# Attention with a token and channel mixer: seven of nine channel-mixing chunks in Strassen's form

## The chip, the cores and the metric

The kernel runs on one NeuronCore of a Trainium2 chip. The metric is the device time of one execution in microseconds (us). The engines are TensorE (PE in the views, with its weight loads as PEld), VectorE (DVE), ScalarE (ACT), GpSimd (POOL) and SyncE (SP), which issues the DMAs.

## The reference

A causal attention with decay feeds a token mixing and a channel mixing, both with a residual. B = 8 batches, H = 8 heads, S = 576 tokens, D = 64; d_model is 512, d_tok 256, d_ch 1536; everything is fp32.

```python
decay = cum[:, :, :, None] - cum[:, :, None, :]          # cum: running sum of log f
scores = np.where(causal, -1000000000.0, scale * q @ k^T + decay)
attn = softmax(scores) @ v
x = np.ascontiguousarray(attn.transpose(0, 2, 1, 3)).reshape(B, S, H * D)
h = np.maximum(x.transpose(0, 2, 1) @ w_tok1, 0.0) @ w_tok2
u = x + h.transpose(0, 2, 1)
h2 = np.maximum(u @ w_ch1, 0.0) @ w_ch2
return u + h2
```

## The kernel before, in words

**Precision.** Each fp32 operand is held as a high part (rounded to the type that PE multiplies fast, by ACT, helper L572) and a low part (the rest, by DVE, L581 and L584, or by POOL, L578). A product of two operands is three matmuls: high weight by high data, low by high, high by low.

**The attention stage**, some 640 us, runs over 64 heads. For each head the scores go into PSUM (L848), DVE takes the row minimum with the mask added (L855), ACT the exponential (L862), POOL normalizes (L890), PE transposes the probabilities (L904) into PSUM, ACT and DVE split them into high and low (L572, L581), and PE multiplies them by v (L974 to L986) into an accumulator that is folded into x (L1024, L1031). Between these steps stands the mixer of the batch before: transposes of x (L1205), the two products of the token mixing (L1238 to L1241 and the lines behind), and two of the twelve tiles of d_ch of the channel mixing (L1307 and its two neighbours for the first product, L1335 to L1337 for the second, whose sum ACT copies out at L1342). The result of these two tiles is kept in DRAM as `part_d`, u as `u_d`.

**The channel-mixing stage** takes the other ten tiles of d_ch in nine chunks of 512 tokens (`begin`, `up`, `down`, L1070 to L1170). Per chunk, `up` is ten groups of 12 matmuls of 128x512 (L1121 to L1123) into one PSUM bank, from which ACT takes relu and the high part and DVE the low part (L584); `down` is ten groups of 12 matmuls (L1142 to L1144) into four accumulators, which DVE adds to the residual at the chunk's end (L1155). That is 240 matmuls a chunk. `third` decodes the weights of this stage while the first chunks run (L682 and others).

**PSUM** has eight banks, b0 to b7. b0 and b1 are one tile of [128, 1024], `pair0`, that holds scores; b2 and b3 are `pair1`, the attention's accumulator. Their halves are the four accumulators of `down`. b4 to b7 are four tiles `bank4` to `bank7` of [128, 512], which everything of the kind "one" takes in turn: transposes, scores, the mixer's products, `up`.

**What sets the order.** `Plan` (L359) gets every operation with an engine, a cost, a priority and the buffers it uses (`Buf` of a kind; `slots_of` says which pieces of memory serve a kind) and lays out one fixed order for each engine, with a slot for each buffer, by walking through its own clock. The engines then run their orders, and an instruction waits on semaphores for instructions of other engines that use the same tile; those waits are put in when the program is built, from the tiles that its operands belong to, and not by the plan.

Of the kernel before, what the change touches and what calls it, by code (L numbers as in the profile page):

```python
# [15 lines left out]
P = 128  # L16
# [323 lines left out]


# [19 lines left out]
class Plan:  # L361
# [9 lines left out]
    FIFO = ("ring", "xt", "part", "pr", "hl", "k1", "k2", "vv", "raw", "vr", "p34", "p2", "p1", "p0", "low", "hid", "d_raw", "d_g", "qf", "f34", "f2", "f1", "f0")  # L371
# [35 lines left out]
    def run(self, slots):  # L407
# [30 lines left out]
        def place_all(o):  # L438
            got, taken, nx = [], set(), {}
            for b in o.bufs:  # L440
                if b.slot is not None:
                    continue
                k = b.kind
# [4 lines left out]
                for s in slots[k]:  # L448
                    if all(free_at(u, o.eng) <= t and u not in taken for u in s):
                        break  # L450
                else:
                    return None
                got.append((b, s))
                taken.update(s)
            return got

        while left:
            moved = False
            for e, lst in ready.items():
# [71 lines left out]
def build(nc, env, dims):  # L531
# [112 lines left out]
    def decode(prio, loads, w, hi, lo, tok, late=None):  # L644
# [35 lines left out]
        def s6():  # L680
# [4 lines left out]
        p.op("DVE", d_dve(w, True), prio, s2, wr=[gb], bufs=[gb], port=True)  # L685
        p.op("DVE", d_dve(w, True), prio, s3, rd=[gb], wr=[(gb, 1)], bufs=[gb], port=True)
        p.op("DVE", d_dve(w), prio, s4, port=True, rd=rd, wr=[(gb, 1)], bufs=[rb, gb])
        p.op("DVE" if late else "POOL", d_dve(w) if late else d_ptt(w), prio, s5, port=True, rd=[(gb, 1)], wr=[gb], bufs=[gb])
        p.op("DVE", d_dve(w), prio, s6, port=True, rd=rd, wr=[gb], bufs=[rb, gb])
# [3 lines left out]
            rd=[gb, (tok, "h")], wr=[(tok, "l")], bufs=[gb], port=True,  # L693
# [7 lines left out]
    def dec_list():  # L701
# [31 lines left out]
        def rest(i, which):  # L733
            def go(prio):
# [3 lines left out]
                else:  # L738
# [4 lines left out]
                    late=f"gate{int(i >= PAIRS0)}",  # L743
# [300 lines left out]
    DB = PRM["DB"] if F1 else 0  # L1044
    whole = [(x * HS, HS, True) for x in range(2 * DB)]
    rest_, n_ch = N - DB * S, -(-(N - DB * S) // 512)
    cuts = [DB * S + x * rest_ // n_ch for x in range(n_ch + 1)]
    part_ = [(x, y - x, False) for x, y in zip(cuts, cuts[1:])]
    chunks = part_ + whole if PRM["DLAST"] else whole + part_
# [20 lines left out]
    def begin(g, ch):  # L1070
# [16 lines left out]
        hl = [(Buf("ring"), Buf("ring")) for c in range(NC)]  # L1087
# [14 lines left out]
    hid = {}  # L1102

    def up(g, ch, i):
# [5 lines left out]
        hid[ch, i] = hb  # L1110

# [15 lines left out]
        p.op("PE", [mm_(w_)] * 12, base + g, mm, rd=[(x, z) for x in ws for z in "hl"] + both, wr=[ps], bufs=[ps, *both, hb])  # L1127
# [3 lines left out]
    def down(g, ch, i):  # L1131
# [4 lines left out]
        for c in range(NC):  # L1136
# [10 lines left out]
            p.op("PE", [mm_(w_)] * 3, base + g + 1.5, mm, rd=[(wk, "h"), (wk, "l"), (hb, 0), (hb, 1)], wr=[acc[c]], bufs=[acc[c], hb])  # L1147
# [15 lines left out]
    steps = [(ch, i) for ch, x in enumerate(chunks) for i in range(0 if x[2] else F1, NF)]  # L1163
    for g, s_ in enumerate(steps):
        if g == 0:
            up(0, *s_)
        if g + 1 < len(steps):
            up(g + 1, *steps[g + 1])
        down(g, *s_)
    return p  # L1170


# [188 lines left out]
def slots_of():  # L1361
# [6 lines left out]
    for kind in ("raw", "vr", "hl", "k1", "k2", "vv", "pr", "p34", "p2", "p1", "p0", "low", "ring", "part", "xt", "d_raw", "d_g"):  # L1368
# [11 lines left out]
def attn_mixer_kernel(  # L1380
# [51 lines left out]
    for _ in range(3):  # L1432
        nc.tensor.matmul(E["one"][("b4",)], ident, mask[:, :512], start=True, stop=True)
# [8 lines left out]
    tiles(mixp, "d_raw", [P, C, 2], U32, n_("d_raw"))  # L1442
    tiles(mixp, "d_g", [P, 2, C], U32, n_("d_g"))
    tiles(mixp, "part", [P, S], F32, n_("part"))
# [29 lines left out]
    def swap(x):  # L1474
# [49 lines left out]
```

## Time and profile before

| | |
|---|---|
| median of 3 runs | 1133.28 us (1130.95 to 1133.99) |
| span of the profiled execution | 1133.7 us |
| mean granted clock of TensorE | 0.986 |
| PE busy | 1088.6 us, 96% |
| DVE, ACT, POOL busy | 620.8, 557.9, 525.3 us |
| L1121 to L1123 and L1142 to L1144, 360 matmuls each | 140.0 or 140.1 us each, 389 ns mean |

The profiled execution has no time of its own beside its span; the three runs lie around it. Busy times are of instructions in work; matmuls are pipelined, so that the 389 ns of one overlap the next, and what a matmul adds to a row of them is the pitch from start to start. A view of windows gives the busy time of each engine in each stretch, with the number of instructions in brackets, then the granted clock, the share of the DMA engines and GB/s; restricted to a tile it counts only instructions that touch it. The tile "bank" is bank4 to bank7 together. In the rows of groups stands: line, engine, operation, output and inputs, count, busy us, mean ns, idle time ahead and what ended it. In a timeline a row begins with the start in us and the duration.

### The profile page before, as it was taken

The page shows a single profiled execution, that of the slowest core. Times are in us where ns is not written, and L with a number is a line of the kernel's source. Part 1 is how long each engine was busy: PE and PEld are TensorE (multiplying, and loading weights), DVE is VectorE, ACT ScalarE, POOL GpSimd, SP SyncE. Part 2 cuts the span into 40 slices and gives each one's busy share as a digit, 9 for nine tenths or more (in the row PEclk, how much of TensorE's full clock was granted, in tenths as well). Part 3 has the DMA queues.
Part 4 walks back from the last instruction along what each step waited for, and adds up shares of the span by engine and source line. Part 5 has one row for each costly group of instructions (what it writes and reads, how often), then busy time and mean ns, then how long its engine had stood idle before and what let it go on. Part 6 is the DMA issues. An engine that isn't in the chain of part 4 may idle for free.

```text
span 1133.7 us, 18919 instructions
## 1 busy us (share of the span) xinstructions
PE 1088.6 (96%) x6542; PEld 947.7 (84%) x6542; DVE 620.8 (55%) x1618; ACT 557.9 (49%) x1441; POOL 525.3 (46%) x613
## 2 busy tenths in 40 slices
PE   8988888999999999999998999999999999999998
PEld 5567777899899999889898888888888888888886
DVE  5677687788787787788779894121212121211111
ACT  4676676868788787778786542121111111111110
POOL 4466786768768687687762304130303031211010
PEclk7998999999999999999999999999999999999999
DMA  7576774878677777767752644130303030302011
GB/s 194 132 164 153 164 212 119 220 212 208 164 188 192 201 182 198 184 191 173 192 151 80 210 134 156 48 88 25 112 1 112 1 112 1 112 1 75 19 56 38
DMA packets 70224, 146.67 MB, mean 129 GB/s; under 512 B 10048, under 2 KB 27456, under 8 KB 69104
## 3 DMA queue, kind: packets, MB, share of 16 engines
q1 hardware_dynamic: 70128, 145.45, 47.0%
q8 instruction: 52, 0.85, 0.3%
q14 instruction: 44, 0.36, 0.1%
HBM read 63.46 MB, written 28.31 MB: 81 GB/s over the span
## 4 chain that ended last, share of the span: by engine, by line
PE 76%; DMA 9%; DVE 5%; SPq 3%; POOL 3%; ACT 3%; issue 2%; DVEq 0%; POOLq 0%; ACTq 0%
DMA k<-hl 7%; PE bank L1121 7%; PE bank L1122 7%; PE bank L1123 7%; PE pair L1142 7%; PE pair L1144 7%; PE pair L1143 7%; PE bank L904 6%; PE bank L848 6%; PE pair L848 3%; PE pair L984 2%; PE pair L986 2%; SPq L821 1%; PE bank L1238 1%; PE pair L974 1%
## 5 line engine op out<-in xcount | busy, mean ns | idle before, releaser
L584 DVE SCALAR_TENSOR_TENSOR hid<-bank,hid 128x512 fp32r<-128x512 f32 x90 | 62.2, 691 | 333.5 <-ACT hid L572 332.9
L578 POOL TENSOR_TENSOR ring<-xt,ring 128x512 fp32r<-128x512 f32 (+1 forms) x68 | 91.7, 1364 | 322.9 <-ACT ring L572 322.3
L572 ACT ACTIVATE hid<-bank 128x512 fp32r<-128x512 f32 x90 | 53.9, 599 | 342.3 <-PE bank L1123 342.1
L890 POOL TENSOR_SCALAR pr<-pr,rec 128x576 f32<-128x576 f32 (+4 forms) x320 | 165.0, 536 | 59.1 <-DVE rec L883 36.2
L572 ACT ACTIVATE p<-bank 128x384 fp32r<-128x384 f32 (+3 forms) x300 | 128.2, 474 | 46.4 <-PE bank L904 43.0
L904 PE MATMUL bank<-ident,pr 128*128 128x128 f32 (+1 forms) x960 | 137.0, 276 | 5.6 <-DVE p L581 2.0
L1122 PE MATMUL bank<-ring,w1r 128*128 128x512 f32 x360 | 140.1, 389 | 0.0
L1121 PE MATMUL bank<-ring,w1r 128*128 128x512 f32 x360 | 140.1, 389 | 0.0
L1143 PE MATMUL pair<-hid,w2r 128*128 128x512 f32 x360 | 140.0, 389 | 0.0
L1144 PE MATMUL pair<-hid,w2r 128*128 128x512 f32 x360 | 140.0, 389 | 0.0
L1142 PE MATMUL pair<-hid,w2r 128*128 128x512 f32 x360 | 140.0, 389 | 0.0
L1123 PE MATMUL bank<-ring,w1r 128*128 128x512 f32 x360 | 140.0, 389 | 0.0
L862 ACT ACTIVATE pr<-bank,nmin 128x448 f32<-128x448 f32 (+3 forms) x256 | 118.1, 467 | 40.5 <-DVE nmin L855 38.6
L581 DVE TENSOR_TENSOR p<-bank,p 128x384 fp32r<-128x384 f32 (+1 forms) x180 | 106.3, 595 | 40.6 <-ACT p L572 38.6
L855 DVE CUSTOM_DVE_ANT_0 bank<-bank,mask 128x448 f32<-128x448 f32 (+3 forms) x256 | 107.1, 432 | 36.3 <-PE bank L848 32.7
L904 PEld LDWEIGHTS bank<-ident,pr 128*128 128x128 f32 (+1 forms) x960 | 108.4, 131 | 18.9 <-DVE low L581 3.2
L848 PE MATMUL bank<-k 128*128 128x320 f32 (+1 forms) x480 | 90.0, 315 | 12.3 <-DMA k<-hl 8.9
L848 PEld LDWEIGHTS bank<-k 128*128 128x128 f32 (+1 forms) x480 | 65.4, 182 | 19.9 <-DMA k<-hl 9.0
L1123 PEld LDWEIGHTS bank<-ring,w1r 128*128 128x128 f32 x360 | 67.6, 188 | 14.1
L1143 PEld LDWEIGHTS pair<-hid,w2r 128*128 128x128 f32 x360 | 67.6, 188 | 14.0
L1144 PEld LDWEIGHTS pair<-hid,w2r 128*128 128x128 f32 x360 | 67.6, 188 | 14.0
L1121 PEld LDWEIGHTS bank<-ring,w1r 128*128 128x128 f32 x360 | 67.7, 188 | 13.9
(125 smaller groups left out, 2454.4 us busy)
## 6 DMA issues: line engine op xcount, KB each, us to landing
k<-hl SPq DMA_DIRECT2D x180, 288.0 KB
raw<-in_qk SPq DMA_DIRECT2D x30, 576.0 KB
vr<-in_v SPq DMA_DIRECT2D x32, 320.0 KB
ud<-xt SPq DMA_DIRECT2D x8, 1152.0 KB
pd<-part SPq DMA_DIRECT2D x32, 288.0 KB
out_t<-part SPq DMA_DIRECT2D x36, 256.0 KB
d_raw<-in_w_ch SPq DMA_DIRECT2D x12, 512.0 KB
d_raw<-in_w_ch SPq DMA_DIRECT2D x40, 128.0 KB
```

The lines of the kernel that those rows point to most:

```text
L572: nc.scalar.activation(out, in_, func, scale=scale)
L848: nc.tensor.matmul(ps[:m, of : of + w], k[:, 0, i0 : i0 + m], k[:, 1, j0 : j0 + w], start=(x == 0), stop=(fq or x == 1))
L855: nc.vector.tensor_tensor_reduce(x, x, E["mask"][:m, a : a + w], -1.0 / D**0.5, 3e38, op0=ALU.add, op1=ALU.min, accum_out=E["nmin"][sm][:m ...
L862: nc.scalar.activation(at(pr)[:m, poff[t] : poff[t] + w], at(buf)[:m, of : of + w], AF.Exp, bias=E["nmin"][sm][:m, t : t + 1], scale=-1.0, ...
L890: nc.gpsimd.tensor_scalar(x, x, r, 0.0, op0=ALU.mult, op1=ALU.add)
L904: nc.tensor.transpose(out, at(pr)[:, poff[i] + start[j] : poff[i] + end[j]], E["ident"])
L1121: nc.tensor.matmul(q, wh[:, c, :], h_, start=(c == 0), stop=False)
L1122: nc.tensor.matmul(q, wl[:, c, :], h_, start=False, stop=False)
L1123: nc.tensor.matmul(q, wh[:, c, :], l_, start=False, stop=(c == NC - 1))
L1142: nc.tensor.matmul(q, wh, h_, start=(i == i0), stop=False)
L1143: nc.tensor.matmul(q, wl, h_, start=False, stop=False)
L1144: nc.tensor.matmul(q, wh, l_, start=False, stop=(i == NF - 1))
```

## The change

Two of the nine chunks stay as they are (`CONV = 2`). Seven are computed by `strassen(s)`: the weight matrix and the data of each product are seen as two by two blocks, and seven products of blocks, with sums of blocks, take the place of eight (the form of Strassen's scheme with seven products in `TERMS`). Both matrix products of the chunk are done so. A block of data is 256 tokens wide, so that matmuls are 128x256 where they were 128x512.

In the first product each of the seven terms is made of five groups of six matmuls, each group into half a bank of PSUM. For the first term ACT copies each group out; for the others DVE adds it to one of the four partial results H11 to H22, for one term to two; ACT takes relu of a partial result when it is complete. In the second product a term is 30 matmuls into a whole pair of banks, and DVE adds the sum to one to four quarters of the buffer R, which holds the residual. POOL makes the sums of data blocks, ACT and DVE split them into high and low parts. `prep` makes the sums of weight blocks S1 to S4 once, during the two chunks that stay, on POOL and DVE, each split by ACT and DVE, and puts them where the attention's weights, the spare part of the ring and the old hidden tiles lay.

To make room, memory is laid out anew: the decode buffers become one tile `dd`, in which H11 to H22 lie later; the part buffers one tile `part`, which R takes whole; the attention stage's mixer weights one tile `held`. The eight banks of PSUM become four tiles `pair0` to `pair3` of [128, 1024]; b4 to b7 are their halves. "any" is any half, "two" any whole pair. From the third pair of weights on the decode may run beside POOL (`port`).

The core of the diff:

```diff
+HW = 256
+CONV = 2
...
-    chunks = part_ + whole if PRM["DLAST"] else whole + part_
+    chunks = [(512 * x, 512, False) for x in range(CONV)]
...
+    def prep(w, pr, eng, kind, prio):
...
+        for x, (o_, y, op) in enumerate((("11", "21", ALU.subtract), ("21", "22", ALU.add), ("22", "11", ALU.subtract), ("12", "22", ALU.subtract))):
+            tail(eng, d(HW), prio, lambda o_=o_, y=y, op=op: tt(view(o_), view(o_), view(y), op), rd=[(g, y)], wr=[(g, o_)], bufs=[g])
...
+    for pr in range(PH):
+        prep(1, pr, "DVE" if pr % 2 else "POOL", GT[pr], late - 60 + 4 * pr)
...
+    TERMS = (("11", "A11"), ("21", "A12"), ("T2", "S2"), ("T3", "S3"), ("T4", "A22"), ("T1", "S1"), ("22", "S4"))
+    L = 3.57
+    LO_POOL = (1, 4, 5, 6)
+
+    def strassen(s):
...
+            for pr in range(PH):
+                ps = Buf("any")
...
+                    for c in (0, 1):
+                        cs = slice(c * P, (c + 1) * P)
+                        h_, l_ = v2(at(th))[:, c, :], v2(at(tl))[:, c, :]
+                        nc.tensor.matmul(q, wh[:, cs], h_, start=c == 0, stop=False)
+                        nc.tensor.matmul(q, wl[:, cs], h_, start=False, stop=False)
+                        nc.tensor.matmul(q, wh[:, cs], l_, start=False, stop=c == 1)
...
+                def add(out, a, ps=ps, Hq=Hq):
+                    nc.vector.tensor_tensor(Hq(out), at(ps)[:, :HW], Hq(a), op=ALU.add)
...
+                if k == 0:
+                    tail("ACT", d_act(HW), pp, lambda ps=ps, Hq=Hq: nc.scalar.activation(Hq("21"), at(ps)[:, :HW], AF.Copy), rd=[ps], wr=[(H["21"], pr)], bufs=[ps, H["21"]])
+                for out, a in ((), (("11", "21"),), (("12", "21"),), (("22", "12"),), (("21", "22"),), (("22", "22"), ("12", "12")), (("12", "12"),))[k]:
...
+        def product(k, src, blk, xs):
+            ps = Buf("two")
...
+            to = (QUADS, ("11",), ("12", "21", "22"), ("21", "22"), ("21",), ("12", "22"), ("12",))[k]
+            for q in to:
+                tail(
+                    "DVE", d_dve(512), t2 + L * (k + 1), lambda q=q: nc.vector.tensor_tensor(Rq(q), v(), Rq(q), op=ALU.add),
+                    rd=[ps], wr=[(R, q)], bufs=[ps, R],
+                )
...
+    for s in range(N // 512 - CONV):
+        strassen(s)
...
+    k["any"] = [(f"b{i}",) for i in (4, 5, 6, 7, 0, 1, 2, 3)]
+    k["two"] = pairs
+    k["R"] = [tuple(("part", i) for i in range(4))]
...
-    pairs = [psum.tile([P, 1024], F32, name=f"pair{i}") for i in range(2)]
-    E["sc"] = {("b0", "b1"): pairs[0]}
-    E["av"] = {("b2", "b3"): pairs[1]}
-    E["acc"] = {(f"b{i}",): pairs[i // 2][:, (i % 2) * 512 : (i % 2) * 512 + 512] for i in range(4)}
-    E["one"] = {(f"b{i}",): psum.tile([P, 512], F32, name=f"bank{i}") for i in range(4, 8)}
+    pairs = [psum.tile([P, 1024], F32, name=f"pair{i}") for i in range(4)]
+    E["two"] = {(f"b{2 * i}", f"b{2 * i + 1}"): x for i, x in enumerate(pairs)}
+    E["sc"] = E["av"] = E["two"]
+    E["any"] = {(f"b{i}",): pairs[i // 2][:, (i % 2) * 512 : (i % 2) * 512 + 512] for i in range(8)}
+    E["acc"] = E["one"] = E["any"]
```

How the orders change. Up to about 615 us of the trace of before the instructions of each engine stand in the same order and on the same banks; what differs is the tile that a bank belongs to. bank4 and bank5 are now the halves of pair2, bank6 and bank7 those of pair3. Lines are 13 later for the attention's (L848 is L861, L904 is L917, L572 is L585, L581 is L594), and L1335 is L1587, L1342 is L1594. The names behind the arrow are the inputs; "waits" are the engines whose semaphores the instruction waits for.

PE in the attention, at 512.6 us of the trace. Before:

```order
L986 MATMUL pair1_64<-p341_172,vv1_167 128x256
L1335 MATMUL bank5_66<-ring8_139,w2h_105 128x288 [waits DVE_49]
L1336 MATMUL bank5_66<-ring8_139,w2l_106 128x288
L1337 MATMUL bank5_66<-ring9_140,w2h_105 128x288
L1335 MATMUL bank5_66<-ring10_141,w2h_105 128x288 [waits Activation_49]
...
L1335 MATMUL bank6_67<-ring8_139,w2h_105 128x288 [waits DVE_49]
...
L848 MATMUL bank4_65<-k10_162 128x320 [waits DMAHW2_49,DMAHW0_49,DVE_49]
```

The same place after:

```order
L999 MATMUL pair1_64<-p341_156,vv1_151 128x256
L1587 MATMUL pair2_65<-ring8_130,held_97 128x288 [waits Activation_49]
L1588 MATMUL pair2_65<-ring8_130,held_97 128x288
L1589 MATMUL pair2_65<-ring9_131,held_97 128x288
L1587 MATMUL pair2_65<-ring10_132,held_97 128x288
...
L1587 MATMUL pair3_66<-ring8_130,held_97 128x288 [waits DVE_49]
...
L861 MATMUL pair2_65<-k10_146 128x320 [waits DMAHW2_49,DMAHW0_49,Activation_49]
```

No row has moved. The first matmul into bank 5 waited for DVE, and now waits for ACT, which reads bank 4; the scores into bank 4 waited for DVE, which read bank 4, and now for ACT, which copies bank 5.

ACT at the same place. Before:

```order
L572 ACTIVATE p340_171<-bank5_66 128x384 [waits PE_49]
L572 ACTIVATE p00_176<-bank6_67 64x512 [waits DVE_49,PE_49]
L572 ACTIVATE p20_173<-bank7_68 128x384 [waits PE_49]
L572 ACTIVATE p00_176<-bank7_68 64x64
L572 ACTIVATE p10_175<-bank4_65 128x512 [waits DVE_49,PE_49]
L767 ACTIVATE vv1_167<-vr0_159 128x10x64 [waits DMAHW2_49,PE_49]
L1342 ACTIVATE part0_148<-bank5_66 128x288 [waits DVE_49,PE_49]
```

After:

```order
L585 ACTIVATE p340_155<-pair2_65 128x384
L585 ACTIVATE p00_160<-pair3_66 64x512 [waits DVE_49,PE_49]
L585 ACTIVATE p20_157<-pair3_66 128x384
L585 ACTIVATE p00_160<-pair3_66 64x64 [waits DVE_49]
L585 ACTIVATE p10_159<-pair2_65 128x512 [waits PE_49]
L780 ACTIVATE vv1_151<-vr0_143 128x10x64 [waits DMAHW2_49,PE_49]
L1594 ACTIVATE part_135<-pair2_65 128x288 [waits DVE_49]
```

The order is the same again. The read of 64x64 has a new wait for DVE, which reads the other half of pair3, and the copy at the end now waits for DVE alone, whose instruction there (L594 into p10) reads the other half of pair2 and itself has a new wait for PE.

The first product of a chunk in Strassen's form, on PE and DVE, which has no counterpart before. PE in a term whose groups DVE adds, the first matmuls of its groups:

```order
L1307 MATMUL pair2_65<-ring4_126,w1r1_6974 128x256 [waits Activation_49]
...
L1307 MATMUL pair3_66<-ring4_126,w1r3_7177 128x256 [waits DVE_49]
...
L1307 MATMUL pair2_65<-ring4_126,w1r5_7181 128x256 [waits DVE_49]
...
L1307 MATMUL pair2_65<-ring4_126,w1r7_7185 128x256
...
L1307 MATMUL pair3_66<-ring4_126,w1r9_7189 128x256 [waits DVE_49]
```

Two groups go into the halves of pair2, then one into pair3, and so on; each first one into a pair waits for DVE, which adds what is there.

ACT's copies of the first term of a chunk:

```order
L1323 ACTIVATE dd_134<-pair3_66 128x256 [waits PE_49]
...
L1323 ACTIVATE dd_134<-pair2_65 128x256 [waits DVE_49,PE_49]
L1323 ACTIVATE dd_134<-pair2_65 128x256 [waits PE_49] x3
```

One group of the term lies in pair3 and four in pair2, and each copy waits for PE.

More of the change, by code (lines that the diff above doesn't have):

```diff
@@ L339, with dd_units @@
 F1 = PRM["F1"]
+QUADS = ("11", "12", "21", "22")
+HW = 256
+CONV = 2
+def dd_units(a, n):
+    return tuple(("dd", i) for i in range(a, a + n))
 def asf(ap):
@@ L637, in build, with decode @@
         fill(i)
-    def decode(prio, loads, w, hi, lo, tok, late=None):
+    def decode(prio, loads, w, hi, lo, tok, late=None, port=True):
         rb, gb = Buf("d_raw"), Buf("d_g")
@@ L1086, in begin @@
             of += w
-        hl = [(Buf("ring"), Buf("ring")) for c in range(NC)]
+        hl = [(Buf("ringx"), Buf("ringx")) for c in range(NC)]
         for c in range(NC):
@@ L1100, in begin @@
         st[ch] = (hl, cp, toks, [Buf("acc") for c in range(NC)])
-    hid = {}
+    hid, hids = {}, []
     def up(g, ch, i):
@@ L1161, in down, with tail @@
                 )
-    steps = [(ch, i) for ch, x in enumerate(chunks) for i in range(0 if x[2] else F1, NF)]
+    def tail(*a, **k):
+        return p.op(*a, port=False, **k)
+    steps = [(ch, i) for ch in range(CONV) for i in range(F1, NF)]
+    at_g = lambda g: g + 150 * (g >= F2)
     for g, s_ in enumerate(steps):
@@ L1167, in build @@
         if g + 1 < len(steps):
-            up(g + 1, *steps[g + 1])
-        down(g, *s_)
+            up(at_g(g + 1), *steps[g + 1])
+        down(at_g(g), *s_)
+    PH = F2 // 2
+    late = base + 400
+    held = [((nm, t), z) for nm, n in (("t1", NS), ("w1", NC), ("w2", F1)) for t in range(n) for z in "hl"]
+    held += [(("t2", k, hf), z) for k in range(NT) for hf in range(2) for z in "hl"]
+    tail("POOL", 1, HB + 3, lambda: None, rd=["gate0", "gate1"], wr=["gatec", *held])
+    tail("POOL", 1, HB + 3, lambda: None, rd=[((f"w{w}r", i), z) for w in (1, 2) for i in range(F2) for z in "hl"], wr=["gated"])
@@ L1367, in slots_of @@
     k["one"] = [(f"b{i}",) for i in (4, 5, 6, 7)]
-    for kind in ("raw", "vr", "hl", "k1", "k2", "vv", "pr", "p34", "p2", "p1", "p0", "low", "ring", "part", "xt", "d_raw", "d_g"):
+    k["any"] = [(f"b{i}",) for i in (4, 5, 6, 7, 0, 1, 2, 3)]
+    k["two"] = pairs
+    k["R"] = [tuple(("part", i) for i in range(4))]
+    k["ringx"] = [(("ring", i),) for i in range(8)]
+    k["tr"] = [(("ring", i),) for i in range(5)]
+    k["d_raw"] = [dd_units(4 * i, 4) for i in range(3)]
+    k["d_g"] = [dd_units(12 + 4 * i, 4) for i in range(2)]
+    for i, q in enumerate(QUADS):
+        k["H" + q], k["gt" + q] = [dd_units(5 * i, 5)], [dd_units(5 * i, 4)]
+    for kind in ("raw", "vr", "hl", "k1", "k2", "vv", "pr", "p34", "p2", "p1", "p0", "low", "ring", "part", "xt"):
         k[kind] = [((kind, i),) for i in range(PRM[f"n_{kind}"])]
@@ L1432, in attn_mixer_kernel @@
     for _ in range(3):
-        nc.tensor.matmul(E["one"][("b4",)], ident, mask[:, :512], start=True, stop=True)
+        nc.tensor.matmul(E["any"][("b4",)], ident, mask[:, :512], start=True, stop=True)
     def tiles(pool, kind, shape, dt, n):
@@ L1481, in swap @@
             tiles(wp, "hid", [P, 2, 512], F32R, PRM["n_hid"])
+            spare = wp.tile([P, 512], F32R, name="spare")
             wp.tile([P, 8], F32, name="even1")
+            early = [held[:, i * 512 : (i + 1) * 512] for i in range(held.shape[1] // 512)]
+            early += [spare[:, :]] + [E["ring"][(("ring", i),)][:, :512] for i in (8, 9, 10, 11)]
+            last = [E["ring"][(("ring", i),)][:, :512] for i in (6, 7)]
+            last += [x[:, j, :] for x in E["hid"].values() for j in (0, 1)]
+            E["piece"] = [("gatec", x) for x in early] + [("gatee", x) for x in last]
     E["swap"] = swap
```

232 lines of the change are left out of this document (203 added, 29 removed).

## The prediction

> **What bounds the kernel now.** I read the page's busy times and the cores first, then the windows of 100 us, then the same windows for the tile bank alone, then single rows.
>
> ```profile
> PE 1088.6 (96%) x6542; PEld 947.7 (84%) x6542; DVE 620.8 (55%) x1618; ACT 557.9 (49%) x1441; POOL 525.3 (46%) x613
> core 0: 1133.7 us, clock 0.986
> ```
>
> Windows, all work (stretch, us, then PE, PEld, DVE, ACT, POOL, clock, DMA share, GB/s):
>
> ```profile
> 300.00:400.00 100.00, 99.10 (x762) 95.03 (x761) 79.56 (x233) 80.66 (x227) 71.20 (x84) 1.00 0.68 182
> 640.00:700.00 60.00, 60.00 (x274) 50.05 (x273) 49.54 (x89) 25.84 (x44) 9.27 (x8) 1.00 0.42 136
> 700.00:760.00 60.00, 60.00 (x267) 49.69 (x266) 11.00 (x17) 9.99 (x18) 16.42 (x14) 1.00 0.30 92
> ```
>
> TensorE (PE) bounds both stages. From about 640 us the nine chunks run with PE full and the others nearly idle. Before, in the attention, PE is busy 99.10 of 100, but VectorE (DVE) and ScalarE (ACT) stand at 80: there the three live by handing PSUM banks around quickly. So I ask two questions: what the chunks save on PE, and whether the banks are still handed around as fast. The profiled execution is the 1133.7 us span; the median of the runs, 1133.28, is 0.4 lower, and I sum against 1133.7 without correcting.
>
> **Seven products for eight.** A chunk has 240 matmuls of 128x512 now and 420 of 128x256 then. The pitch of the first is 60 / 267 = 0.2247 us (700 to 760 above), so 53.9 us a chunk. That of the second is in the attention, where six such matmuls stand in a row:
>
> ```profile
> 320.48 0.28 PE L1238 MATMUL bank<-ring,t1h 128*128 128x256 f32 x1
> ...
> 321.08 0.29 PE L1241 MATMUL bank<-ring,t1h 128*128 128x256 f32 x1
> ```
>
> Five pitches are 0.60, so 0.12 each and 50.4 us a chunk: 3.5 less, times seven **-25 us**. A rounding of 0.0025 in the pitch is 1 us a chunk, so -32 to -18. The Trainium skill (TensorE: Matmul & The Clock Gate, "Wait — 56ns, not 53.3ns?") has a warm matmul at its columns over 2.4 GHz plus 2.5 ns; by that a chunk would go from 51.8 to 45.9 us and the seven would save 41. This trace is slower than that rule by 9 to 11 ns a matmul in both sizes, so the row stands.
>
> The other engines must feed this. The nearest rows:
>
> ```profile
> L581 DVE TENSOR_TENSOR ring<-bank,ring 64x256 fp32r<-64x256 f32 x16 | 6.7, 418 | 1.3 <-ACT ring L572 0.9
> L584 DVE SCALAR_TENSOR_TENSOR hid<-bank,hid 128x512 fp32r<-128x512 f32 x90 | 62.2, 691 | 333.5 <-ACT hid L572 332.9
> L572 ACT ACTIVATE hid<-bank 128x512 fp32r<-128x512 f32 x90 | 53.9, 599 | 342.3 <-PE bank L1123 342.1
> L572 ACT ACTIVATE ring<-bank 64x256 fp32r<-64x256 f32 x16 | 6.0, 376 | 0.1
> L578 POOL TENSOR_TENSOR ring<-xt,ring 128x512 fp32r<-128x512 f32 x36 | 46.0, 1298 | 303.6 <-ACT ring L572 303.4
> L578 POOL TENSOR_TENSOR w1l<-d_g,w1h 128x256 fp32r<-128x256 f32 x4 | 2.9, 735 | 2.0 <-ACT w1h L572 1.9
> ```
>
> DVE per chunk: 35 adds out of PSUM and 35 low parts at 0.418, 3 low parts and 14 adds at 0.691: 41 us. ACT: 60 operations of 256 at 0.376 and 7 of 512 at 0.599: 27. GpSimd (POOL): 20 of 512 at 1.298 and 4 of 256 at 0.735: 29. All fit under 50 us of PE: no bound by load. The residual's buffer R is single, so its load waits for the chunk before to store its last quarter, but is needed only when the first matrix product, 210 matmuls or 25 us, is done: nothing. The weight combinations (ten preparations, about 29 us of DVE and 33 of POOL) fall into the two chunks kept, of some 54 us each, where DVE has 10.5 and then 49 free of 60, POOL 44: hidden, **+2** (0 to 8, if the decode before them is late). At the end one add follows the last matmul in place of four: **-1**.
>
> **The PSUM tiles.** The diff also makes bank4 to bank7 halves of two pair tiles, and that reaches into the attention. What sharing a tile does is visible now, in the last chunk, whose accumulators are halves of pairs:
>
> ```profile
> 1126.69 0.39 PE L1144 MATMUL pair<-hid,w2r 128*128 128x512 f32 x1
> 1127.37 0.39 PE L1144 MATMUL pair<-hid,w2r 128*128 128x512 f32 x1
> 1127.87 2.65 DVE L1155 TENSOR_TENSOR part<-pair,part 128x512 f32<-128x512 f32 x4 [2.83 <-PE pair L1144]
> ```
>
> The first add needs only the half finished by 1127.08 (1126.69 + 0.39), but starts 0.11 after the other half's last matmul ends at 1127.76. Two engines take turns on a pair, whichever halves they touch. In the changed order the attention's instructions stand in the same order as before, but have such waits on pair2 and pair3, as the rows ahead show. One turn, in the trace of before:
>
> ```profile
> 512.17 1.07 ACT L572 ACTIVATE p<-bank 128x384 fp32r<-128x384 f32 x3
> 512.71 0.30 PE L1335 MATMUL bank<-ring,w2h 128*128 128x288 f32 x1
> 513.37 0.30 PE L1337 MATMUL bank<-ring,w2h 128*128 128x288 f32 x1
> 513.57 0.67 DVE L581 TENSOR_TENSOR p<-bank,p 128x512 fp32r<-128x512 f32 x1
> 513.75 0.40 ACT L1342 ACTIVATE part<-bank 128x288 f32<-128x288 f32 x1
> 514.54 0.40 PE L848 MATMUL bank<-k 128*128 128x320 f32 x1
> ```
>
> The third ACT operation reads bank 4 until 513.24; the six matmuls fill bank 5 beside it; DVE reads bank 4, ACT copies bank 5, the scores go into bank 4. As halves of one pair they queue. With 0.05 us for a handoff (a choice; the add above took 0.11), the matmuls start at 513.29 (+0.58), the sixth ends 0.58 later than its 513.67, DVE starts at 514.30 (+0.73), ACT at 515.02 (+1.27), the scores at 515.47 (+0.93). Queued behind that wait on PE is everything, since PE goes in order: transposes, the other heads' products, then ACT and DVE that wait for these.
>
> I carried this rule by hand along all the rows of two stretches, each instruction starting when its own engine and its new and old predecessors allow, with the durations of before:
>
> ```profile
> 349.73 0.60 PE L904 MATMUL bank<-ident,pr 128*128 128x128 f32 x4
> 369.56 0.29 PE L1307 MATMUL bank<-ring,w1h 128*128 128x288 f32 x1
> 510.36 0.49 PE L904 MATMUL bank<-ident,pr 128*128 128x128 f32 x3
> 529.12 0.38 PE L1205 MATMUL bank<-ident,xt 128*64 128x128 f32 x2
> ```
>
> PE comes out 7.4 us late after 19.8 us, and 7.5 after 18.8: 0.38 and 0.40 us per us. The second had 5.0 after its first half, so halves differ (0.53, 0.26). I take 0.39, with 0.30 to 0.46. Over what stretch it holds I read from the load of the bank tiles alone (same columns, without POOL):
>
> ```profile
> 0.00:100.00 100.00, 50.45 (x267) 34.19 (x267) 37.37 (x80) 36.33 (x121) 0.92 0.67 169
> 100.00:200.00 100.00, 59.91 (x400) 51.67 (x400) 48.39 (x106) 44.22 (x138) 0.94 0.61 156
> 200.00:300.00 100.00, 81.36 (x585) 74.19 (x586) 56.58 (x124) 53.99 (x169) 1.00 0.80 211
> 300.00:400.00 100.00, 83.62 (x600) 75.34 (x599) 59.53 (x131) 59.04 (x181) 1.00 0.68 182
> 400.00:500.00 100.00, 80.23 (x570) 71.59 (x569) 58.72 (x129) 54.92 (x167) 0.98 0.72 185
> 500.00:600.00 100.00, 80.36 (x573) 71.42 (x572) 59.27 (x133) 58.80 (x186) 1.00 0.66 173
> 600.00:640.00 40.00, 34.94 (x245) 32.71 (x246) 12.21 (x26) 10.30 (x26) 1.00 0.48 157
> ```
>
> From 200 to 600 the four are alike. From 300 to 400 PE, DVE and ACT together hold banks for 202 us: taken in turns on two pairs, 101 of 100, before a single handoff. So the two pairs are full even if packed perfectly, and an order that was made for four banks doesn't pack. 400 us at 0.39: **+156** (120 to 184). From 100 to 200 the two pairs carry 76 of 100: half the rate, **+20** (10 to 35). Before that 62: **+10** (0 to 20). After 600, 29 of 40: **+6** (0 to 12). Together +192, 130 to 251.
>
> In the chunks in Strassen's form the same rule costs at two kinds of place. In the first product ACT copies each group of six matmuls, and the next group goes into the same pair: its last matmul starts at 0.60 and ends at 0.88, ACT reads from 0.93 to 1.30, PE goes on at 1.35 where 0.72 was due. 0.63 lost, four times. In the products with one add, two groups in one pair alternate with one in the other: from the last matmul's start the pair is free after 0.28 + 0.05 + 0.34 + 0.42 + 0.05 = 1.14, PE is back after seven pitches, 0.84: 0.30 lost in every three of 25 groups. The 0.34 is an add's 0.418 less the overlap of two in a row, from these:
>
> ```profile
> 647.60 0.68 DVE L581 TENSOR_TENSOR w1r<-d_g,w1r 128x512 fp32r<-128x512 f32 x1
> 648.20 0.69 DVE L682 SCALAR_TENSOR_TENSOR d_g<-d_raw,d_g 128x512 uint32<-128x512 uint32 x1
> ```
>
> That is 2.5 + 2.5, plus about 0.5 for the product with two adds and 1 that I allow for low parts in DVE's row (no row shows it): 6.5 a chunk, times seven **+45** (0, if PE finds the pairs free, to 65). The second matrix product gathers in whole pairs, each summed while PE fills another: nothing. The stage nets +20 (-30 to +45).
>
> Sum: 1133.7 + 192 + 45 - 25 + 2 - 1 = **1347**.
>
> **The rivals.** *The waits mostly fall into gaps.* Then only the load counts: 1 to 10% over the dense 400 us, some +40, and +15 elsewhere: 1133.7 + 55 + 20 + 1 = 1210. For it: idle is left on DVE and ACT (80 of 100). Against: PE has none (99.10), and each wait on PE is paid. Chance 0.10.
>
> *The halves stay free.* If a wait on the other half has always been met when it is reached, before's pace holds: 1133.7 - 25 + 1 = 1110, faster. Its place is the attention; it decides if those waits cost less than 25 us over 600, 0.04 per us. Against it stands the add at 1127.87. Chance 0.04, and 0.02 for a cost of the waits that ends near that point. The Trainium skill (PSUM — Partial Sum Buffer, "PSUM bank collisions raise a hardware error") has two engines on different banks running clean, so the chip does not ask for these turns; here the add's row shows the program asking for them.
>
> *PE cools.* With PE at 99.10 / 1.39 = 71 of 100 the clock may be taken back. The rows speak both ways:
>
> ```profile
> 100.00:110.00 10.00, 8.30 (x51) 7.00 (x51) 6.95 (x24) 7.55 (x25) 5.62 (x7) 0.77 0.22 50
> 150.00:160.00 10.00, 8.32 (x62) 7.28 (x60) 8.46 (x26) 7.17 (x18) 7.82 (x12) 1.00 0.81 245
> ```
>
> At a clock of 0.8 PE's part of the turns (83.62 of 202, 0.41) takes a quarter longer: 10% of some 570 us, +57, so 1404. Chance 0.06. The Trainium skill (TensorE: Matmul & The Clock Gate, "A second HAM failure mode: psum-queue depth-cycling") has short idle times between groups making the clock swing; the first row agrees, the second does not.
>
> **How the numbers follow.** The forecast has 0.78. Its bounds, added as independent (-62 to +59 in the attention, -50 to +25 in the chunks), give 1267 to 1411; I allow 10 more on each side, since the rate rests on two stretches of 19 us out of 400. The range of 1255 to 1420 holds the cooled case and leaves out the other two, 0.16. The chances of faster, same and slower by over 0.3% come from the same cases: the halves that stay free are faster, what ends near them falls half to faster and half to no change, all others are slower. About 0.3% is what a measurement of this kernel can tell from no change. Faster 0.05, same 0.01, slower 0.94.
>
> **What would show it.** In the profile after: the chunks kept as before begin near 835 us instead of 640; PE in 300 to 400 is busy about 71 of 100, and its idle time stands before writes to pair2 and pair3, released by DVE and ACT; a chunk in Strassen's form takes about 57 us for 53.9, its idle time in the first product and in those with one add, none in the second matrix product. The prediction is wrong if PE stays near 99 in the attention; if a chunk takes 50 us, only the term of 45 falls.

## The result, and the profile after

The changed kernel took 1479.84 us (median of 4 runs, 1468.51 to 1483.51) beside 1133.59 before: 1.304 times as long, 95% interval 1.299 to 1.309. The forecast was slower, 1347, with a range up to 1420: the side was right, the size too small by 133 us. The busy times of the page and the cores, after:

```profile
PE 1217.4 (82%) x7802; PEld 1044.0 (70%) x7802; DVE 942.3 (64%) x2193; ACT 720.3 (49%) x1852; POOL 699.9 (47%) x761
core 0: 1481.4 us, clock 0.931
```

PE's share fell from 96 to 82%, and its clock from 0.986 to 0.931. Where the time went is read from four marks. The chunks that stayed as they were begin at 908.8 us where the chunks began at 636.8 before; they end at 1038.8; the seven in Strassen's form end at 1477.5. Before, the last matmul ends at 1129.1, so that the last seven chunks, 53.9 us each, begin at 751.6, and the first two, with the attention's last matmuls among theirs, took 114.8. So the attention lost 272 us, the two old chunks took 130.0 for 114.8 (+15), and the seven took 62.7 each for 53.9 (+61): 348, the difference of the two spans. These are the three places to explain; the term for each was +192, +2 and +20.

Windows of all work after: three of the attention, the two old chunks, and the first and the second matrix product of one chunk in Strassen's form (stretch, us, PE, PEld, DVE, ACT, POOL, clock, DMA share, GB/s):

```profile
100.00:200.00 100.00, 75.53 (x486) 63.10 (x486) 57.21 (x167) 50.79 (x138) 53.50 (x68) 0.83 0.47 122
300.00:400.00 100.00, 76.98 (x506) 65.86 (x505) 58.98 (x163) 54.90 (x150) 49.73 (x62) 0.97 0.56 147
700.00:800.00 100.00, 78.78 (x465) 66.97 (x464) 51.02 (x149) 54.58 (x150) 46.72 (x61) 0.85 0.49 122
908.80:1038.80 130.00, 117.99 (x498) 94.37 (x499) 91.59 (x146) 39.75 (x82) 54.11 (x48) 0.96 0.25 78
1163.41:1194.35 30.94, 27.37 (x206) 25.08 (x205) 15.88 (x39) 12.22 (x30) 11.88 (x11) 1.00 0.27 82
1194.35:1225.01 30.66, 27.59 (x207) 26.45 (x206) 29.49 (x48) 14.78 (x37) 17.06 (x14) 0.94 0.06 19
```

In the attention no engine is full any more: PE has 77 of 100 where it had 99, DVE and ACT 59 and 55 where they had 80. That is the picture of engines that wait for each other. In a new chunk the two halves differ: in the first product DVE is half idle (15.88 of 30.94) and PE waits all the same; in the second DVE is full, 29.49 of 30.66.

The place whose order stands ahead of the prediction, in the timeline of after, ACT, DVE and PE apart:

```profile
716.16 0.70 ACT L585 ACTIVATE p<-pair 64x64 fp32r<-64x64 f32 x2 [0.75 <-DVE low L594]
...
718.80 0.41 ACT L1594 ACTIVATE part<-pair 128x288 f32<-128x288 f32 x1 [1.31 <-DVE p L594]
```

```profile
718.08 0.69 DVE L594 TENSOR_TENSOR p<-pair,p 128x512 fp32r<-128x512 f32 x1 [0.99 <-PE pair L1589]
```

```profile
716.91 0.40 PE L1587 MATMUL pair<-ring,held 128*128 128x288 f32 x1 [0.88 <-ACT p L585]
...
719.26 1.14 PE L861 MATMUL pair<-k 128*128 128x320 f32 x7 [0.18 <-ACT part L1594]
```

It is the queue that was worked out: ACT's read of one half ends at 716.86, PE starts in the other half at 716.91, DVE follows PE, ACT follows DVE at 718.80, and the scores follow ACT at 719.26. From ACT's end to the scores it is 2.40 us, where it was 1.30 before (513.24 to 514.54) and 2.23 was worked out.

### The profile page after: what moved, and what is told of

Its sections match the earlier page's. It is cut to its first block, busy times and chain, and to the rows that moved or that the text cites. A ratio compares the mean times of both kernels' runs of the same rounds, so it can differ in the third digit from the quotient of the medians.

```text
span 1481.4 us, 23124 instructions
## 1 busy us (share of the span) xinstructions
PE 1217.4 (82%) x7802; PEld 1044.0 (70%) x7802; DVE 942.3 (64%) x2193; ACT 720.3 (49%) x1852; POOL 699.9 (47%) x761
## 4 chain that ended last, share of the span: by engine, by line
PE 57%; DVE 22%; ACT 12%; issue 6%; DMA 1%; POOL 0%; SPq 0%; DVEq 0%; ACTq 0%; POOLq 0%
PE pair L917 6%; PE pair L861 6%; ACT pr L875 5%; PE pair L1307 4%; DVE pair L868 4%; PE pair L1395 4%; ACT p L585 4%; PE pair L1393 3%; PE pair L1394 3%; DVE ring L594 3%; DVE p L594 3%; PE pair L1309 3%; PE pair L1308 3%; DVE dd L1317 2%; DVE low L594 2%
## 5 line engine op out<-in xcount | busy, mean ns | idle before, releaser
L875 ACT ACTIVATE pr<-pair,nmin 128x320 f32<-128x320 f32 (+4 forms) x320 | 165.8, 522 | 131.0 <-DVE nmin L868 69.0
L868 DVE CUSTOM_DVE_ANT_0 pair<-pair,mask 128x192 f32<-128x192 f32 (+4 forms) x320 | 155.8, 499 | 99.5 <-PE pair L861 39.8
L917 PE MATMUL pair<-ident,pr 128*128 128x128 f32 (+1 forms) x960 | 151.4, 291 | 68.4 <-ACT pr L875 15.8
L585 ACT ACTIVATE p<-pair 128x384 fp32r<-128x384 f32 (+3 forms) x300 | 132.0, 473 | 129.7 <-PE pair L917 63.8
L917 PEld LDWEIGHTS pair<-ident,pr 128*128 128x128 f32 (+1 forms) x960 | 107.9, 137 | 106.8 <-issue 25.7
L594 DVE TENSOR_TENSOR p<-pair,p 128x384 fp32r<-128x384 f32 (+1 forms) x180 | 107.4, 598 | 106.7 <-ACT p L585 66.3
L594 DVE TENSOR_TENSOR ring<-dd,ring 128x256 fp32r<-128x256 f32 x251 | 161.4, 685 | 9.4 <-ACT ring L585 9.4
L861 PE MATMUL pair<-k 128*128 128x320 f32 (+2 forms) x720 | 140.0, 329 | 31.6 <-DVE p L594 6.2
L585 ACT ACTIVATE ring<-dd 128x256 fp32r<-128x256 f32 x251 | 102.2, 414 | 106.9 <-PE pair L1394 98.3
L861 PEld LDWEIGHTS pair<-k 128*128 128x128 f32 (+1 forms) x720 | 107.2, 199 | 48.3 <-DVE p L594 8.3
L1307 PE MATMUL pair<-ring,w1r 128*128 128x256 f32 x280 | 84.3, 301 | 15.5 <-ACT dd L1323 11.7
L585 ACT ACTIVATE ring<-xt 128x512 fp32r<-128x512 f32 (+1 forms) x89 | 57.0, 647 | 71.1 <-PE pair L1308 40.1
L1395 PE MATMUL pair<-ring,w2r 128*128 128x256 f32 x280 | 83.1, 297 | 9.2 <-DVE ring L594 9.2
L594 DVE TENSOR_TENSOR low<-pair,p 64x64 fp32r<-64x64 f32 (+1 forms) x120 | 52.0, 444 | 46.9 <-ACT p L585 13.0
L1393 PE MATMUL pair<-ring,w2r 128*128 128x256 f32 x280 | 79.1, 283 | 0.0
L1308 PE MATMUL pair<-ring,w1r 128*128 128x256 f32 x280 | 79.0, 282 | 0.0
```

What stands on the lines that cost most here:

```text
L585: nc.scalar.activation(out, in_, func, scale=scale)
L594: nc.vector.tensor_tensor(out, in_, asf(hi), op=ALU.subtract)
L861: nc.tensor.matmul(ps[:m, of : of + w], k[:, 0, i0 : i0 + m], k[:, 1, j0 : j0 + w], start=(x == 0), stop=(fq or x == 1))
L868: nc.vector.tensor_tensor_reduce(x, x, E["mask"][:m, a : a + w], -1.0 / D**0.5, 3e38, op0=ALU.add, op1=ALU.min, accum_out=E["nmin"][sm][:m ...
L875: nc.scalar.activation(at(pr)[:m, poff[t] : poff[t] + w], at(buf)[:m, of : of + w], AF.Exp, bias=E["nmin"][sm][:m, t : t + 1], scale=-1.0, ...
L917: nc.tensor.transpose(out, at(pr)[:, poff[i] + start[j] : poff[i] + end[j]], E["ident"])
```

## The experiments

**The PSUM tiles alone.** The kernel before, with this one edit:

```diff
-    pairs = [psum.tile([P, 1024], F32, name=f"pair{i}") for i in range(2)]
+    pairs = [psum.tile([P, 1024], F32, name=f"pair{i}") for i in range(4)]
...
-    E["one"] = {(f"b{i}",): psum.tile([P, 512], F32, name=f"bank{i}") for i in range(4, 8)}
+    E["one"] = {(f"b{i}",): pairs[i // 2][:, (i % 2) * 512 : (i % 2) * 512 + 512] for i in range(4, 8)}
```

> The kernel before with one part of the change alone: the four tiles bank4 to bank7 become halves of pair2 and pair3; no chunk in Strassen's form, no other memory moved. Theory (two engines take turns on a pair, in the attention): the chunks begin near 905 us instead of 637, as in the changed kernel, and the time is about 1400 (1380 to 1425), since the nine old chunks keep their 54 us each. Theory of the cooled clock as a cause of its own in the changed kernel's new chunks or layout: no loss here, 1134. If only part of the 272 us is the pairs', the rest must be the merged tiles in SBUF, and the time lies between.

Measured: 1398.58 us, 1.235 times before (1.227 to 1.244); the chunks begin at 889.8 us. Its window from 300 to 400, and the transposes L904 there and before, in the groups by line:

```profile
300.00:400.00 100.00, 78.28 (x498) 67.44 (x497) 59.91 (x158) 53.96 (x149) 48.24 (x60) 0.93 0.54 142
```

```profile
L904 PE MATMUL bank<-ident,pr 128*128 128x128 f32 (+1 forms) x960 | 137.0, 276 | 5.6 <-DVE p L581 2.0 <-DVE low L581 1.7 <-ACT pr L862 1.0
```

```profile
L904 PE MATMUL pair<-ident,pr 128*128 128x128 f32 (+1 forms) x960 | 150.2, 289 | 67.2 <-ACT pr L862 15.0 <-DVE low L581 12.2 <-DVE p L581 10.4
```

The first row of L904 is before's, the second is of this kernel. The idle time of PE ahead of the transposes went from 5.6 to 67.2 us, and what ends it is DVE or ACT. The attention stage lost 253 of the 272 us without any chunk in Strassen's form, and with no buffer of SBUF moved. Of the other 19, 12 arise at the attention's end, in the instructions that stand behind 615 us in the trace of before, where this kernel loses 1; what they are is seen with the banks given back. The first two chunks lost another 7 here: from the first `up` to the third chunk's first `down` it is 123.5 us for 116.7.

**One pair.** The same with bank4 and bank5 as one pair, bank6 and bank7 single.

> The kernel before with bank4 and bank5 as halves of one pair, bank6 and bank7 tiles of their own. Theory of the turns: some 100 us more than before (60 to 160), less than half of the loss with two pairs, because the free banks let the rows that wait be fewer and PE stays busier, so that the clock should be taken back less (mean over 0.95). Rival, that the loss is one of tile tracking as such and not of load: half of it, about 135.

Measured: 1324.81 us, 1.170 times (1.162 to 1.178); the chunks begin at 816.1, 179 us late. The clock was over 0.95, as expected (0.973), but neither figure for the time was met: one pair costs some seven tenths of what two cost. A reason can be read from the load of the bank tiles over the attention, before and then here, where only bank6 and bank7 still have this name:

```profile
0.00:636.80 636.80, 467.67 (x3220) 408.41 (x3221) 332.08 (x724) 317.03 (x980) 0.98 0.68 178
0.00:816.00 816.00, 234.38 (x1432) 190.73 (x1432) 160.07 (x335) 157.47 (x457) 0.96 0.53 139
```

The two free banks take 1432 of the 3220 matmuls, so the shared pair takes the other 1788. By the 202 us for two pairs of the prediction, it is as full as it was with two. That one full pair is enough to hold an engine whose instructions stand in a fixed order is a reading; no run tests it.

**The banks given back.** The changed kernel with bank4 to bank7 as tiles of their own:

```diff
-    k["two"] = pairs
+    k["two"] = pairs[:2]
...
-    pairs = [psum.tile([P, 1024], F32, name=f"pair{i}") for i in range(4)]
+    pairs = [psum.tile([P, 1024], F32, name=f"pair{i}") for i in range(2)]
...
+    E["any"].update({(f"b{i}",): psum.tile([P, 512], F32, name=f"bank{i}") for i in range(4, 8)})
```

> The changed kernel with bank4 to bank7 as tiles of their own again (halves of a bank pair only for b0 to b3; whole pairs for the second product only from b0 to b3). Theory of the turns: the chunks begin near 637 us, the first product of a chunk in Strassen's form falls from 31.0 to about 25.5 us, the second stays at 31.5, the two old chunks keep their loss of 22: about 637 + 130 + 7 x 57 + 4 = 1170 (1150 to 1190), still slower than before. Rival, that merged tiles in SBUF cost too: the chunks begin well after 640.

Measured: 1174.11 us, 1.036 times before (1.030 to 1.042). The first and second product of a chunk:

```profile
830.91:855.44 24.53, 24.53 (x207) 24.53 (x206) 16.85 (x38) 12.02 (x29) 11.61 (x10) 1.00 0.35 109
855.44:887.42 31.98, 27.22 (x206) 26.27 (x205) 29.83 (x49) 15.02 (x38) 17.25 (x14) 0.95 0.05 17
```

The first product is now full on PE; the second is no faster (31.98 for 30.66). With the tiles in SBUF still merged, the attention is back: against the same instructions of before PE is 1.4 us late at 615 us, so merged tiles in SBUF cost nothing that shows. But the chunks begin at 648.0, 11 late. Timeline, DVE, POOL and PE, of what stands between:

```profile
629.27 1.66 DVE L683 TENSOR_SCALAR dd<-dd 128x512 uint32<-128x512 uint32 x1
630.96 1.79 DVE L687 SCALAR_TENSOR_TENSOR dd<-dd 128x512 f32<-128x512 uint32 x1
...
635.80 0.41 DVE L683 TENSOR_SCALAR dd<-dd 128x512 uint32<-128x512 uint32 x1
636.13 0.68 DVE L695 SCALAR_TENSOR_TENSOR dd<-dd 128x512 uint32<-128x512 uint32 x1
636.73 0.68 DVE L687 SCALAR_TENSOR_TENSOR dd<-dd 128x512 f32<-128x512 uint32 x1
```

```profile
629.00 6.32 POOL L591 TENSOR_TENSOR ring<-xt,ring 128x576 fp32r<-128x576 f32 x4 [9.28 <-ACT ring L585]
```

```profile
641.50 0.61 PE L1587 MATMUL bank<-ring,held 128*128 128x288 f32 x1 [6.46 <-DVE ring L597]
```

VectorE's decode, which the diff lets run beside GpSimd, took 1.66 us for 0.41 and 1.79 for 0.68 while GpSimd was at work, and PE waited 6.46 us for the low part behind it. In no_sums and sums_dve below PE loses 11 in the same place; in the three later runs whose plan keeps the decode off GpSimd's time it loses nothing, and port_plan begins its chunks at 636.3. The two halves of the loss nearly add up: 267 us from the tiles alone (0.235 of 1133.6) and 41 left without them are 308 of 345 (0.304). The rest, 37, is put down to the waits on pairs in the new chunks' first products, which only the two changes together have (31.7 us for 25.2, seven times, would be 45). What is left here is 41 us in a kernel whose PE saves 25 on matmuls, so something else costs 66: the 10 of the decode are part of it.

**GpSimd's sums left out.** As banks_back, without the twelve sums of hidden blocks that GpSimd makes per chunk (so the second product works on blocks that were not summed), and with a cost of next to nothing for them in the plan:

```diff
-                    nc.gpsimd.tensor_tensor(v(o2), v(x2), v(y2), op=op)
+                    pass
```

> As banks_back, with GpSimd's sums of hidden blocks (T1 to T4 in the second product) left out, so that part of the computation is missing. Theory of the shared work of VectorE and GpSimd (VectorE's low parts out of SBUF take 0.42 us alone and 1.24 while GpSimd runs): the low parts fall to 0.42 to 0.5 in the mean, the second product from 31.5 to about 26 us, the whole about 40 us under banks_back. Rival, that VectorE is late because it waits for ScalarE's high parts or has too much work in itself: the second product stays over 30.

Measured: 1134.07 us, 1.004 times before (1.000 to 1.009), 40 under banks_back. The low parts in the groups of the new chunks, banks_back first, then this kernel, and the second product of this kernel:

```profile
L594 DVE TENSOR_TENSOR ring<-dd,ring 128x256 fp32r<-128x256 f32 x248 | 171.0, 726 | 10.9 <-ACT ring L585 8.9
L1317 DVE TENSOR_TENSOR dd<-bank,dd 128x256 f32<-128x256 f32 x244 | 94.5, 418 | 32.8 <-PE bank L1309 32.2
```

```profile
L594 DVE TENSOR_TENSOR ring<-dd,ring 128x256 fp32r<-128x256 f32 x248 | 114.4, 487 | 20.6 <-ACT ring L585 19.0
```

```profile
852.78:877.98 25.20, 25.07 (x206) 24.63 (x205) 21.65 (x49) 15.05 (x38) 1.96 (x2) 1.00 0.06 21
```

DVE's low part with both inputs in SBUF fell from 726 to 487 ns in the mean; its add of the same shape with one input in PSUM was 418 all along. The second product lost 6.8 us and is nearly full on PE. So what the second products lose, 6.8 us each and 47 in all, is GpSimd running beside VectorE, not the waits on ScalarE. The edit also takes away every wait for the sums themselves, but these were not the limit: in the waits of banks_back's second product (855.4 to 887.4) no instruction of PE, DVE or ACT is released by GpSimd, and DVE is busy 29.83 of 31.98. How two operations meet is seen in the changed kernel, DVE and then POOL, count and total of several in a row:

```profile
1195.23 7.89 DVE L594 TENSOR_TENSOR ring<-dd,ring 128x256 fp32r<-128x256 f32 x7
...
1215.32 1.42 DVE L594 TENSOR_TENSOR ring<-dd,ring 128x256 fp32r<-128x256 f32 x4
```

```profile
1196.76 9.61 POOL L1356 TENSOR_TENSOR dd<-dd 128x512 f32<-128x512 f32 x8
...
1210.78 1.53 POOL L1281 TENSOR_TENSOR xt<-xt,xt 128x512 f32<-128x512 f32 x1
```

Seven low parts beside GpSimd take 1.13 us each; four without it 0.36. Counted over the changed kernel's new chunks, 69 low parts lay wholly inside GpSimd's work and took 1.14 us in the mean (up to 1.52), where the expectation has 1.24: 14 of them, which began in the last 0.15 us of one of GpSimd's operations, took 0.41 to 0.43, the other 55 took 1.33. The 135 that met no work of GpSimd took 0.418; 105 adds out of PSUM wholly beside GpSimd took 0.420, as alone. GpSimd is hardly slowed: its sum of 128x512 took 1.39 us beside low parts, for 1.30. The Trainium skill (SBUF — State Buffer, "SBUF: two separate sides") says that VectorE with two inputs in SBUF and GpSimd share one pair of ports by an exclusive lock, so that one blocks the other for its whole instruction. The rows here agree in that VectorE is held, and in that an input from PSUM escapes it. That GpSimd is blocked as long in its turn they do not show: it lost 0.09 us a sum.

**Three ways around it.** The sums on VectorE; a plan that lets no SBUF work of VectorE run beside GpSimd (`port=True` on weight sums, low parts and decode); both.

```diff
-                    nc.gpsimd.tensor_tensor(v(o2), v(x2), v(y2), op=op)
+                    nc.vector.tensor_tensor(v(o2), v(x2), v(y2), op=op)
```

> As banks_back, with the twelve sums of hidden blocks per chunk on VectorE in place of GpSimd. Theory of the shared work: the low parts of the second product fall from 0.72 to near 0.42 us, VectorE gets 7 us of sums a chunk (8 at 0.69, 4 at 0.42) and has some 48 us of work in 50.4; the second product falls from 31.8 to 26 to 29 us, the whole 20 to 40 us under banks_back, 1135 to 1155. Rival, that VectorE's own work is the bound: the second product stays at 31 or grows.

Measured: 1161.32 us, 1.026 times before (1.021 to 1.030), 13 under banks_back, less than expected. The second product of two chunks takes 29.2 and 29.4 us:

```profile
847.41:876.61 29.20, 25.55 (x207) 24.72 (x205) 28.24 (x62) 14.87 (x38) 1.91 (x2) 1.00 0.05 19
1016.88:1046.25 29.37, 25.68 (x207) 24.79 (x205) 28.41 (x62) 15.04 (x38) 2.09 (x2) 1.00 0.06 19
```

DVE is busy 28.24 of 29.20. The low parts are fast (485 ns in the mean), but the 45 us of DVE's work in a chunk are unevenly laid: 16.9 in the first product, 28.2 in the second, where 25.2 are to be had. The expectation summed over the chunk and missed that; the rival named the cause, though not the time (it had 31 or more).

```diff
-        return p.op(*a, port=False, **k)
+        return p.op(*a, **k)
...
+                    rd=[(H[q], pr), (x, 0)], wr=[(x, 1)], bufs=[x, H[q]], port=True,
```

> As banks_back, with the order laid out by a plan that lets no operation of VectorE that has both inputs in SBUF run beside GpSimd (weight sums, low parts, decode), sums still on GpSimd. Theory: fewer low parts meet GpSimd, so the two old chunks lose less than 15 us and the second product falls below 31.8; but 29 us of GpSimd and 17 of VectorE that exclude each other must fit in 50.4 a chunk, the sums in the second half of it: 1130 to 1165. Rival, that the engines drift from the plan and meet all the same: 1170 as banks_back.

Measured: 1187.35 us, 1.050 times (1.044 to 1.057), outside what was expected. The old chunks did get their time back (111.3 for 114.8), but the weight sums moved into the first new chunk, whose first product waited 20 us for a low part:

```profile
636.20:747.50 111.30, 111.30 (x500) 92.56 (x500) 85.46 (x143) 41.86 (x80) 47.79 (x44) 1.00 0.32 102
747.50:794.90 47.40, 27.07 (x212) 26.84 (x210) 35.35 (x67) 19.46 (x48) 23.54 (x20) 0.78 0.20 67
```

The later second products stayed at 33 us. Both together:

> Both: the plan that keeps VectorE's SBUF work off GpSimd's time, and the sums on VectorE. Theory: the least time of the three, 1115 to 1140, since the loss of the old chunks (15 us) and that of the second products (45) both shrink; if VectorE's 48 us in 50.4 are too many, as sums_dve.

Measured: 1162.55 us, 1.025 times (1.021 to 1.030): as sums_dve, the second products at 29.3, and the first new chunk late by 22 us. The figure of 1115 to 1140 was not met; the other branch of the expectation, "as sums_dve", is what came. That the work which may not overlap is too much for the time beside two old chunks is a reading that no run tests.

**A version without the second product.** What the runs left standing is the first product in Strassen's form: 25.2 us for 27.0, full on PE, with DVE adding out of PSUM. So: the banks given back, Strassen's form in the first product, the second as before, half the weight sums, and the plan of port_plan, which keeps VectorE's work in SBUF off GpSimd's time. The edit of the second product:

```diff
-    for pr in range(PH):
-        prep(2, pr, "DVE" if pr % 2 else "POOL", GT[PH + pr], late - 30 + 4 * pr)
...
+                    nc.tensor.matmul(q, wh, h_, start=j == 0, stop=False)
+                    nc.tensor.matmul(q, wl, h_, start=False, stop=False)
+                    nc.tensor.matmul(q, wh, l_, start=False, stop=j == F2 - 1)
+
+                tail("PE", [mm_(512)] * 3, pp + 1.5, mm, rd=[(x, n) for x in (xh, xl) for n in (0, 1)] + [((f"w2r", 2 * pr + a), y) for y in "hl"], wr=[acc[c]], bufs=[acc[c], xh, xl])
```

> A version that the runs point to: bank4 to bank7 as tiles of their own, and Strassen's form in the first matrix product alone (24.5 us for seven terms, then ten steps of 12 matmuls of 128x512 as before, 27.0); no sums of hidden blocks, half the weight sums, laid out by the plan that keeps VectorE's SBUF work off GpSimd's time. Theory: a chunk takes 52.2 us for 53.9, seven of them save 12; VectorE has some 28 us of work a chunk, so nothing waits; if the five weight preparations fit beside the decode in the two old chunks the whole is 1120 to 1126 for some 1132, else up to 1140. Rival, that ScalarE and VectorE can't split the hidden blocks in time at the turn from the first product to the second, 1 to 2 us a chunk: no gain.

Measured: 1118.41 us beside 1129.49, 0.992 times before (0.988 to 0.995), as expected: a gain of under 1%, but clear of no change. One chunk:

```profile
842.08:867.30 25.22, 25.22 (x211) 25.22 (x210) 17.05 (x43) 13.44 (x34) 14.18 (x11) 1.00 0.40 126
867.30:894.53 27.23, 27.23 (x122) 22.55 (x121) 8.74 (x21) 7.41 (x20) 1.29 (x1) 1.00 0.00 1
```

52.45 us for 53.9, PE full in both halves; seven times 1.5 is 10, and the ratio is worth 10 (6 to 13).

## Why the prediction was wrong

The forecast was 133 us short. Of these 80 lie in the attention (272 for 192), 13 in the two old chunks (15 for 2) and 41 in the new ones (61 for 20).

**The waits of the attention were right, and near their size.** Two engines take turns on a pair: shown by pairs_only and banks_back, one adding it and one taking it away. The attention lost 272 us where the term had 192 (130 to 251). Set against the same instructions in the trace of before, PE is 53 us late at 200 us (the term had 30), 251 at 600 (186), 272 at the start of the chunks (192). In the two stretches that were walked by hand the rate came out at 0.44 and 0.46 us per us for 0.38 and 0.40; over the 400 us it was 0.50, outside "I take 0.39, with 0.30 to 0.46". What that step left out is the clock of PE. After 600 us it is 21 for 6, and 12 of these are the decode beside GpSimd.

**PE's clock was made a rival, and came on top.** This is the step that failed in the attention: the cooled clock was priced at +57 beside the forecast with a chance of 0.06, as if one excluded the other. The attention as a whole, before and after:

```profile
0.00:636.80 636.80, 596.29 (x4364) 539.85 (x4365) 492.21 (x1413) 468.60 (x1289) 438.63 (x545) 0.98 0.68 178
0.00:908.80 908.80, 709.06 (x4364) 584.89 (x4364) 526.62 (x1426) 486.49 (x1293) 436.72 (x545) 0.90 0.48 126
```

In these traces the granted clock is either 1.0 or 0.5; it stood at 0.5 for 31 of the 636.8 us before and for 181 of the 908.8 after. Those of the attention's instructions on PE that follow each other without a gap in both executions are 71 us further apart in total after, start to start, and 58 of the 71 fall on instructions run at 0.5. The other 201 of the 272 us stand where PE has a gap in one of the two. Up to 600 us the part at 0.5 is 52 of the 251: the rest, 199, is near the 186 of the term. From 200 to 600 it is 35 of 198, and the rest is 0.41 per us, inside the range that was taken; from 100 to 200 it is 14 of 36, and the rest, 22, is near the +20. Both stretches walked by hand stood at 1.0 all through in the trace of after. So the clock cost about 58. That the 57 is so near is partly luck, as it came from a clock of 0.8 and the mean was 0.90. All this is read from the two traces and not shown by an experiment: none kept the clock at 1.0 with the waits in place, and a gap at 0.5 is counted here as a wait. 192 + 57 with the other terms is the 1404 of that rival, still 76 short.

**"All fit under 50 us of PE: no bound by load" failed.** This is the step that failed in the chunks. It took 0.418 for each low part, a row of an operation that reads PSUM. With both inputs in SBUF and GpSimd at work it was 1.14 in the mean; and the step summed a chunk where the second product alone has 25 us. The sign that the second product has no idle time on PE did not come. This was worth 6.2 us a chunk after (31.4 with the six matmuls at its edge, for 25.2), 43 in all, where the prediction had nothing. The diff lifts the plan's `port` flag for all this work (`tail` passes `port=False`), so that the plan lets VectorE run beside GpSimd; that was not priced.

The two old chunks ("hidden, +2") lost 15 us in the changed kernel, by two causes. The shared pairs alone cost 7 there in pairs_only. GpSimd beside VectorE is the likely cause of the 8 lost in banks_back (648.0 to 771.1): six low parts of weights took 7 us beside GpSimd, and PE waited 4.35 us for the adds behind them in DVE's row; in port_plan, where the weight sums were moved out, these 8 were gone. With the 10 of the decode at the attention's end and the 47 of the second products these 8 make the 66 of banks_back but for 1. Timeline of banks_back, DVE, POOL, PE:

```profile
706.55 7.08 DVE L594 TENSOR_TENSOR held<-dd,held 128x256 fp32r<-128x256 f32 x6 [5.01 <-ACT held L585]
713.56 0.68 DVE L1164 TENSOR_TENSOR part<-pair,part 128x512 f32<-128x512 f32 x1
```

```profile
706.75 4.34 POOL L1105 TENSOR_TENSOR part<-part,xt 128x512 f32<-128x512 f32 x3
```

```profile
715.58 0.76 PE L1151 MATMUL pair<-hid,w2r 128*128 128x512 f32 x1 [4.35 <-DVE part L1164]
```

**The first product was right.** 6.5 us a chunk were forecast from the waits on pairs; it took 31.7 for 25.2, and 25.2 when the banks were given back. The copies of the first term are spaced 1.44 us where 1.35 was worked out:

```profile
1165.05 0.38 ACT L1323 ACTIVATE dd<-pair 128x256 f32<-128x256 f32 x1 [0.81 <-PE pair L1309]
1166.49 0.38 ACT L1323 ACTIVATE dd<-pair 128x256 f32<-128x256 f32 x1 [1.06 <-PE pair L1309]
```

The four waits at the copies come to 2.8 us in this chunk (2.5 forecast), and a wait for an add where two groups share a pair is 0.29 (0.30 forecast). Of the 6.5, 1 was an allowance without a row, so that the sum met is partly luck.

**The matmul gain was right.** 210 matmuls at 0.12 us are the 25.2 us that a product took wherever nothing waited (the first product in banks_back, no_sums and first_only), as the row of the attention said.

The rivals that had the waits fall into gaps or never bind are refuted by pairs_only.

## What to carry to other kernels

A change of how memory is cut into tiles is a change of who waits for whom, wherever those tiles are used; look at the added waits of the whole program before pricing the new part. Cost an operation from a row with the same operands in the same memories and with the same engines at work beside it, and sum it over the stretch in which it must be done, not over the loop. Where a forecast leaves TensorE waiting, its granted clock is part of the forecast and not a rival to it: here it fell from 0.98 to 0.90 in the attention while the waits cost their own time.

## What the runs showed that was not expected

One shared pair among the four banks cost seven tenths of what two cost (179 of 253 us in the attention). VectorE's operation of 128x256 with both inputs in SBUF took 0.418 us alone and 1.14 in the mean beside GpSimd, while GpSimd's sum of 128x512 took 1.39 for 1.30; the same shape with an input in PSUM took 0.420 either way.
